# Convolution, routing and loads of a convolution-then-MoE kernel regrouped: sequences in place of half sequences, and another mix of block sizes

## The chip, the cores and the metric

The kernel runs on one core of one Trainium2 chip. The metric is the time of the core in device microseconds for one launch. The kernel before took 1353.02, 1347.88 and 1350.54 us in three runs; their median is 1350.54 us. Everything is in fp32.

The names of the engines: TensorE (PE in the profile; PEld is its weight load), VectorE (DVE), ScalarE (ACT), GpSimd (POOL) and SyncE (SP, which here only issues DMAs).

## The reference

Eight sequences of 3584 tokens with 192 channels go through a causal convolution of seven taps, whose weights are shared by the 24 channels of a head, and then through a mixture of eight experts in which each token uses one expert.

```python
# lightweight convolution: weight is (8 heads, 7 taps)
w = softmax(weight, axis=-1)
x_pad = concatenate([zeros(B, 6, D), x], axis=1)
out[b, s, h, :] = sum_k w[h, k] * x_pad[b, s + k, h, :]       # heads of 24 channels

# experts, x is now the convolution's output
logits = x @ w_gate                                            # (B, S, 8)
local_gate = sigmoid(x @ w_local)
for b in range(B):
    prev_e = -1
    for s in range(S):
        fresh_e = argmax(logits[b, s])
        e = fresh_e if s == 0 or local_gate[b, s] < 0.5 else prev_e
        prev_e = e
        p = softmax(logits[b, s])
        out[b, s] = p[e] * (relu(x[b, s] @ w1[e]) @ w2[e])     # 192 -> 1024 -> 192
```

A token with an open local gate takes over the expert of the token before it, so routing is a scan along the sequence. The expert's two products are nearly all of the arithmetic.

## The kernel before

**Tokens and parts.** The 28672 tokens are cut into 16 parts of `PT` = 1792, two (`PER`) for each sequence. In a part each of the 128 partitions holds `NT` = 14 consecutive tokens, and a load of a part brings six more tokens per partition (`HALO`) for the taps. `load_x` (L129) issues such a load on SP's queue, 1920 KB.

**Parts 0 and 1** are convolved on TensorE in the opening (`wide`, L210, and `wide_route`, L410), so that the first experts can start early. Nothing of that is looked at here, except that `route1`, the routing of part 1, is emitted to its end (L1254) before the first block's products.

**Parts 2 to 15** go through `conv` (L383). For each of eight heads ScalarE multiplies the first tap (L394, 128 x 336 elements) and VectorE adds the other six, one `scalar_tensor_tensor` each (L404), in place in a row tile `y_sb` in SBUF: 48 VectorE instructions per part. `ys` holds four row tiles (L111), one for each part. At the fifth head the load of the next part is issued (L401), into the other one of two buffers `xs`.

`logits` (L581) then turns the rows with four VectorE transposes (L586), multiplies by the gates on TensorE (L597, 48 small products), brings the result back with ScalarE (L602), another transpose (L605) and sixteen small copies (L613). `route` (L618) is some fifty small VectorE instructions on 14 or 112 elements per partition: which expert, the scan of the local gate over tokens, partitions and parts, the softmax, and for each token its row in a table `slots` in DRAM, where tokens of one expert lie together. `tables` (L771) follows: for each kind of block, `table` (L808) works out in 18 to 22 tiny VectorE instructions which expert and rows each block takes. 

**Scatters.** A routed part leaves fourteen entries in `to_put`. `put` (L788) takes one and lets GpSimd write 128 rows to `slots` with an indirect DMA (L795), ordered behind a given ScalarE instruction. The places of these calls are written into the loops of the blocks.

**Blocks.** The experts work on blocks of 128, 256 or 512 rows of one expert (1, 2 or 4 units). How many of each kind are certain to be full after each part is worked out when the kernel is built (`ONE`, `TWO`, `FOUR`, L64 to L67): units of 128 until part `EARLY`, 256 until part `FIRST`, then 512, and at the end pairs and single units for what is left (L912 to L916). For each block `load_w` (L926) brings the expert's weights, 1536 KB, into one of four buffers, and `load_rows` (L936) its rows from `slots`; the latter waits for the scatters of the parts that it needs. `ensure` (L1206) does this up to three blocks ahead; when a part needed soon isn't yet routed and put, it forces steps of its work.

A block of 128 or 256 rows is `hidden` (L989: products L1000, ReLU on ScalarE L1004, scatters behind it) and `output` (L1077: products L1089, ScalarE's scaled copy L1097, VectorE's scaled add L1101, GpSimd's indirect store of 128 rows L1106). A block of 512 rows uses `seven` (L1032) in place of `hidden`: seven half-size products (L1048) in place of eight by the method of Strassen and Winograd, with sums made by GpSimd before (`combine_w`, `combine_x`, L1009 to L1030), copies by ScalarE (L1053, L1057, L1059) and sums by VectorE (L1062, L1065, L1072) between them. Meanwhile the rows of the next block are turned (`turn_out`, `turn_in`, L376 and L978).

**The order.** It is written out by hand: what a function emits first runs first on its engine. Convolution and routing are generators, which emit one VectorE instruction and yield its estimated price in us. `step(time)` (L1150) is called at fixed places in a block and draws work from them until the given time is spent, routing before convolution; "pe" and "hop" mark places where routing must wait for a free PSUM bank or for another engine, and convolution fills the gap. A block of 512 calls `step` four times:

```python
SIDE = (3.6, 4.6, 3.6, 3.6)
LEAD = 2
```

`step(SIDE[0])` stands ahead of L1062, `step(SIDE[1])` ahead of `output`, and the other two ahead of the two passes of L1101. Smaller blocks call it with 2.1, 1.2 and 1.3 us (128 rows) or 4.6, 1.2 and 3.6 us (256 rows). Convolution of a part starts (`start_conv`, L1121) when its predecessor's is done, when it is no more than `LEAD` parts ahead of routing, and when no scatter of the part three before waits:

```python
free = not any(p[0] <= g - 3 for p in to_put)
```

## Time and profile before

| what | value |
|---|---|
| median of three runs | 1350.54 us |
| the profiled execution's own time | 1407.22 us |
| its span in the profile | 1405.5 us |
| mean granted clock of TensorE | 0.98 |
| VectorE, convolution's taps (L404), 672 instructions | 398.1 us, mean 604 ns |
| ScalarE, first taps (L394), 112 instructions | 63.1 us, mean 581 ns |
| GpSimd, scatters to `slots` (L795), 228 instructions | 228.2 us, mean 1001 ns |
| GpSimd, stores of the output (L1106), 229 instructions | 231.6 us, mean 1011 ns |
| TensorE, `output` (L1089) / `hidden` (L1000) | 636.0 us / 354.2 us |
| DMA: weights, 112 loads of 1536 KB and 12 of 512 KB; tokens, 14 loads of 1920 KB | 201 GB/s over the span |

The profiled execution took 56.7 us longer than the median of the runs without a profile. The durations in the profile belong to the profiled execution, so a sum of them is to be compared with 1407.22 us. A group of instructions is named by its line, its engine, its operation and its tiles; busy time is the sum over the span, and instructions on different engines overlap.

### The profile page before, as it was taken

What the parts mean: (1) busy time and instruction counts of PE and PEld (TensorE: products, weight loads), DVE (VectorE), ACT (ScalarE), POOL (GpSimd) and SP (SyncE); (2) the same over time, 40 slices, a digit from 0 to 9 for tenths busy, and PEclk for the clock granted to TensorE, in tenths of its full rate; (3) what the DMA queues carried; (4) which work ended last, traced back from release to release, by engine and by line L of the source; (5) the groups of instructions that cost most, each with busy time, mean ns of one, the idle gap of its engine ahead of it and who ended that gap; (6) DMA issues with size and microseconds to landing.
All of it is one profiled execution on the core that took longest, in us unless ns stands there. A gap on an engine that the chain in (4) does not pass through costs nothing.

```text
span 1405.5 us, 41143 instructions
## 1 busy us (share of the span) xinstructions
PE 1323.0 (94%) x16474; PEld 1247.0 (89%) x16474; DVE 925.4 (66%) x2556; ACT 681.7 (49%) x1441; POOL 655.3 (47%) x759
## 2 busy tenths in 40 slices
PE   9799999899999999998989999989999799999997
PEld 8789999899989999897878887878889689999997
DVE  6879889698888978889999898995721122110000
ACT  5355555444444544445564645444444355544543
POOL 4445353343434444356665665664656644512111
PEclk9999999999999999999999999999999989999999
DMA  5799998875657666562543524233242243335893
GB/s 195 270 379 353 355 377 314 339 278 191 223 205 271 240 211 243 196 259 92 195 157 104 192 85 159 73 130 118 88 152 85 88 151 125 107 132 196 304 338 132
DMA packets 60197, 284.70 MB, mean 203 GB/s; under 512 B 11744, under 2 KB 30999, under 8 KB 43874
## 3 DMA queue, kind: packets, MB, share of 16 engines
q1 hardware_dynamic: 37680, 236.81, 47.1%
q0 software_dynamic: 22320, 45.22, 8.7%
q8 instruction: 132, 2.16, 0.6%
q14 instruction: 63, 0.52, 0.1%
q10 hardware_dynamic: 2, 0.00, 0.0%
HBM read 236.39 MB, written 46.07 MB: 201 GB/s over the span
## 4 chain that ended last, share of the span: by engine, by line
PE 75%; DVE 17%; issue 3%; ACT 2%; DMA 1%; another core or an unknown queue 0%; POOL 0%; DVEq 0%; POOLq 0%; ACTq 0%; SPq 0%
PE ps L1089 36%; PE ps L1000 23%; PE ps L1048 11%; DVE y_sb L404 6%; PE ps L376 2%; PE ps L597 1%; DVE lt L613 1%; DVE h L1065 1%; DMA xg<-slots 1%; DVE h L1062 1%; DVE o_sb L1101 1%; DVE h L1072 1%; ACT h L1057 1%; PE hps L226 1%; ACT h L1053 0%
## 5 line engine op out<-in xcount | busy, mean ns | idle before, releaser
L1089 PE MATMUL ps<-wb,h 64*128 64x192 f32 x7328 | 636.0, 326 | 8.5 <-issue 6.9
L1089 PEld LDWEIGHTS ps<-wb,h 64*128 64x128 f32 x7328 | 605.3, 188 | 16.3 <-issue 12.8
L1106 POOL DMA_INDIRECT out_dram<-o_sb,xg x229 | 231.6, 1011 | 455.0 <-DVE o_sb L1101 396.5
L404 DVE SCALAR_TENSOR_TENSOR y_sb<-x_sb,c,y_sb 128x336 f32<-128x336 f32 x672 | 398.1, 604 | 30.3 <-ACT y_sb L394 13.1
L1000 PE MATMUL ps<-xT,wb 64*128 64x128 f32 (+1 forms) x4320 | 354.2, 314 | 4.4 <-issue 2.3
L1000 PEld LDWEIGHTS ps<-xT,wb 64*128 64x128 f32 x4320 | 332.8, 188 | 16.2 <-issue 7.7
L795 POOL DMA_INDIRECT slots<-y_sb,posi x228 | 228.2, 1001 | 226.7 <-ACT h L1073 77.9
L1101 DVE SCALAR_TENSOR_TENSOR o_sb<-ps,xg,o_sb 128x192 f32<-128x192 f32 x229 | 87.3, 413 | 309.5 <-ACT o_sb L1097 303.4
L1097 ACT ACTIVATE o_sb<-ps,xg 128x192 f32<-128x192 f32 x229 | 86.8, 418 | 323.0 <-PE ps L1089 316.3
L1004 ACT ACTIVATE h<-ps 128x256 f32<-128x256 f32 (+1 forms) x360 | 148.2, 464 | 193.0 <-PE ps L1000 112.8
L978 ACT COPY xT<-ps 128x128 f32<-128x128 f32 (+2 forms) x464 | 194.1, 418 | 13.7 <-PE ps L376 4.4
L1048 PE MATMUL ps<-xT,wb 64*128 64x256 f32 x1248 | 151.9, 382 | 1.9 <-POOL xT L1026 1.2
L1048 PEld LDWEIGHTS ps<-xT,wb 64*128 64x128 f32 x1248 | 125.3, 191 | 14.1 <-POOL xT L1026 1.6
L376 PEld LDWEIGHTS ps<-ident,xg 64*64 64x64 f32 (+1 forms) x916 | 47.5, 127 | 30.4 <-DVE h L1062 21.7
L1048 PE MATMUL ps<-xc,wt 64*128 64x256 f32 x416 | 56.0, 387 | 18.0 <-ACT h L1057 14.1
L376 PE MATMUL ps<-ident,xg 64*64 64x64 f32 (+1 forms) x916 | 53.2, 224 | 20.9 <-DVE h L1062 16.0
L1062 DVE TENSOR_TENSOR h<-ps,h 128x1024 f32<-128x1024 f32 x26 | 31.6, 1217 | 58.2 <-PE ps L1048 56.1
L1048 PEld LDWEIGHTS ps<-xc,wt 64*128 64x128 f32 x416 | 39.2, 187 | 28.6 <-ACT h L1057 17.7
L394 ACT ACTIVATE y_sb<-x_sb,c 128x336 f32<-128x336 f32 x112 | 63.1, 581 | 0.0
L1048 PE MATMUL ps<-xc,wb 64*128 64x256 f32 x416 | 56.6, 416 | 4.2 <-ACT h L1059 3.8
L1057 ACT COPY h<-ps 128x1024 f32<-128x1024 f32 x26 | 26.3, 1012 | 63.1 <-PE ps L1048 57.6
L1048 PEld LDWEIGHTS ps<-xc,wb 64*128 64x128 f32 x416 | 45.4, 205 | 11.7 <-issue 8.2
(266 smaller groups left out, 1036.1 us busy)
## 6 DMA issues: line engine op xcount, KB each, us to landing
wb<-in_w_dram SPq DMA_DIRECT2D x112, 1536.0 KB
x_sb<-in_x_dram SPq DMA_DIRECT2D x14, 1920.0 KB
xg<-slots SPq DMA_DIRECT2D x26, 390.0 KB
xg<-slots SPq DMA_DIRECT2D x35, 195.0 KB
wb<-in_w_dram SPq DMA_DIRECT2D x12, 512.0 KB
xg<-slots SPq DMA_DIRECT2D x53, 97.5 KB
out_dram<-o_sb,xg POOLq DMA_INDIRECT x229
slots<-y_sb,posi POOLq DMA_INDIRECT x228
```

The source lines that it names most:

```text
L376: nc.tensor.transpose(to, src[rows], identity=ident[rows, rows])
L394: nc.scalar.activation(cols(h), chans(h, 0), Act.Copy, scale=c[:, h, 0:1])
L404: nc.vector.scalar_tensor_tensor(cols(h), chans(h, k), c[:, h, k:k + 1], cols(h), Alu.mult, Alu.add)
L795: ins = nc.gpsimd.indirect_dma_start(out=slots[:, :], in_=rows, in_offset=None, out_offset=bass.IndirectOffsetOnAxis(ap=to, axis=0)).ins
L978: copied = nc.scalar.copy(a, b)
L1000: nc.tensor.matmul(hps[:, half, j, :], lhsT=wb[rows, f0:f0 + P], rhs=xT[rows, d, :], start=(d == 0 and j == 0), stop=(d == KD - 1), skip_g ...
L1004: relu = nc.scalar.activation(hT[two][:, half], hps[:, half], Act.Relu)
L1048: nc.tensor.matmul(to[:, half, j, :], lhsT=b[rows, j * P:(j + 1) * P], rhs=a[rows, :], start=(first and j == 0), stop=True, skip_group_che ...
L1089: nc.tensor.matmul(yps[:, half, k * D:(k + 1) * D], lhsT=h[two][rows, side, j, k * P:(k + 1) * P], rhs=wb[rows, WA + f * D:WA + (f + 1) * ...
L1097: nc.scalar.activation(o_sb[:, k, :], yps[:, 0, k * D:(k + 1) * D], Act.Copy, scale=xg[:, at + k, 0:1])
L1101: nc.vector.scalar_tensor_tensor(o_sb[:, k, :], yps[:, 1, k * D:(k + 1) * D], xg[:, at + k, 0:1], o_sb[:, k, :], Alu.mult, Alu.add)
L1106: sent = nc.gpsimd.indirect_dma_start(out=out, in_=o_sb[:, k, :], in_offset=None, out_offset=bass.IndirectOffsetOnAxis(ap=xg.bitcast(I32)[ ...
```

## The change

1. *Groups.* The parts from the fifth on are convolved, routed and tabled two at a time, that is, by sequences. `GROUPS` is 0, 1, 2, 3, 5, 7, ..., 15: a sequence has the number of its second part. `NS` = 28 tokens per partition in place of 14. Convolution has 28 x 24 = 672 elements in each instruction, routing 28 or 224; the charges (`yield`) grow from 0.6 to 1.0 for a tap and by 0.12 for most steps of `route`. `logits` still transposes and multiplies part by part, and joins the two at the transpose of L605 and the copies of L613. The scan of the local gate then never crosses a part inside a sequence.
2. *Loads.* The tokens lie in memory as (sequence, half of the heads, token, 96 channels). A load brings half of the heads of a part (parts 2 and 3) or of a sequence, and convolution goes by such units (`UNITS`). It is issued in the third of the four heads of the unit before it. The extra load at block `LATE` = 3 is gone, and `LEAD` too.
3. *Row tiles.* `ys` has two tiles of twice the size in place of four. A convolution starts when the scatters of the sequence two before have been emitted.
4. *Blocks.* `EARLY` goes from 3 to 4 and `FIRST` from 8 to 6.
5. *Scatters.* `more` emits a second `put` while more than 14 rows wait, after the three places in `seven` and after the ReLUs in `hidden`.
6. *Budgets.* `SIDE` is (3.0, 4.0, 3.0, 3.0). The last part of `route1` (the tables of part 1) is emitted after the first block's `output`, and that block has other budgets.

The diff, cut to its core:

```diff
-EARLY = 3
+EARLY = 4
...
-FIRST = 8
+FIRST = 6
...
+GROUPS = [*range(EARLY)] + [*range(EARLY + 1, NPART, 2)]
+ONE = {g: _sure(min(g + 1, EARLY) * PT, UT) for g in GROUPS}
...
-    ys = ctx.enter_context(tc.tile_pool(name="ys", bufs=4))
+    ys = ctx.enter_context(tc.tile_pool(name="ys", bufs=2))
...
+    def load_x(g, hh):
+        x_sb = x_tile()
+        n, skip = (NT, g % PER * PT) if g < EARLY else (NS, 0)
+        src = x[g // PER, hh]
+        win = bass.AP(tensor=src.tensor, offset=src.offset + skip * DH,
+                      ap=[[n * DH, P], [1, (n + HALO) * DH]])
+        nc.sync.dma_start(out=x_sb[:, :n + HALO, :].rearrange("p t d -> p (t d)"), in_=win)
         return x_sb
...
-        return ys.tile([P, NB, DG], F32, name="y_sb")
+        return ys.tile([P, 2 * NB, DG], F32, name="y_sb")
...
+    def conv(u, x_sb):
+        g, hh = UNITS[u]
+        if hh == 0:
+            got[g] = rows_in(g)
+        y_sb = got[g]
+        n = NT if g < EARLY else NS
...
-        first(0)
+        heads = range(hh * H // 2, (hh + 1) * H // 2)
+        first(heads[0])
         yield 0
-        for h in range(H):
-            if h + 1 < H:
+        for h in heads:
+            if h + 1 in heads:
                 first(h + 1)
-            if h == H // 2 and 2 < g < NPART - 1:
-                x_in[g + 1] = load_x(g + 1)
+            if h == heads[2] and u + 1 < len(UNITS):
+                x_in[UNITS[u + 1]] = load_x(*UNITS[u + 1])
             for k in range(1, KC):
...
-                yield 0.6
+                yield 0.6 if n == NT else 1.0
...
+        parts = n // NT
+        ls = sm.tile([P, 2, 2, TQ * Q], F32, name="ls", bufs=1)
...
+        for part in range(parts):
+            zt = z_tile()
...
+            for half in range(2):
+                nc.scalar.copy(ls[:, half, part, :], lps[half])
+            yield "hop"
...
+    def more(behind):
+
+        if len(to_put) > NT:
+            put(behind)
+
+    def puts_by(behind):
+        put(behind)
+        more(behind)
...
             for _ in range(shares[two] if n == 2 else (0, sum(shares))[two]):
                 put(relu)
+            if n == 2 or two:
+                more(relu)
...
-        put(nc.scalar.copy(h11, xb))
+        puts_by(nc.scalar.copy(h11, xb))
...
-        put(nc.scalar.copy(h22, yb))
+        puts_by(nc.scalar.copy(h22, yb))
...
-        put(nc.scalar.activation(h12, h12, Act.Relu))
+        puts_by(nc.scalar.activation(h12, h12, Act.Relu))
...
-            step(1.2 if n < KT else SIDE[2 + part], wps_p if n < KT else None)
+            step((1.2 if n > 1 or st["block"] else 0) if n < KT else SIDE[2 + part],
+                 wps_p if n < KT else None)
...
-    SIDE = (3.6, 4.6, 3.6, 3.6)
-    LEAD = 2
-    LATE = 3
+    SIDE = (3.0, 4.0, 3.0, 3.0)
+    LATER = GROUPS[2:]
+    UNITS = [(g, hh) for g in LATER for hh in range(2)]
...
     def start_conv():
-        g = st["conv"] + 1
-
-        free = not any(p[0] <= g - 3 for p in to_put)
-        if (st["cgen"] is None and g < NPART and g <= st["route"] + LEAD and free
-                and (g != 3 or g in x_in and st["block"] > LATE + 2)):
-            st["conv"] = g
-            st["cgen"] = conv(g, x_in.pop(g))
-            next(st["cgen"])
+        u = st["unit"] + 1
+        if st["cgen"] is None and u < len(UNITS) and UNITS[u] in x_in:
+            last = UNITS[u][0] // PER * PER - PER - 1
+            if st["routed"] >= last and not any(p[0] <= last for p in to_put):
+                st["unit"] = u
+                st["cgen"] = conv(u, x_in.pop(UNITS[u]))
+                next(st["cgen"])
...
-    rest(route1)
+    next(route1)
     start.close()
...
-        if i == LATE:
-            x_in[3] = load_x(3)
...
-        step({1: 2.1, 2: 4.6, 4: SIDE[1]}[n], zps_p if n == KT else xps_p)
+        step(2.4 if i == 0 else {1: 2.1, 2: 4.6, 4: SIDE[1]}[n], zps_p if n == KT else xps_p)
         output(n, wbs.pop(i), xgs.pop(i), hT)
+        if i == 0:
+            rest(route1)
```

The rest of the diff gives the small tiles of `route` 28 columns and takes `n` of them, and lets `tables` and `blocks` run over `GROUPS`.

## The prediction

> **What bounds the kernel now.** I read the page first, then stretches of the span one by one, then the chain of waits in two of them, then single blocks. The first two lines are the page's shares and its slices of 1/40 of the span.
>
> ```profile
> PE 1323.0 (94%) x16474; PEld 1247.0 (89%) x16474; DVE 925.4 (66%) x2556; ACT 681.7 (49%) x1441; POOL 655.3 (47%) x759
> PE   9799999899999999998989999989999799999997
> DVE  6879889698888978889999898995721122110000
> DMA  5799998875657666562543524233242243335893
> ```
>
> TensorE is busy throughout, so what the kernel can gain is TensorE's work itself and the few per cent in which it waits. The windows view says where those lie. Its columns are the length, then busy time (and instructions) of PE, PEld, DVE, ACT and POOL, the granted clock, the DMA share and GB/s.
>
> ```profile
> 48.00:262.00 214.00, 202.73 (x3208) 196.88 (x3210) 183.34 (x556) 111.62 (x350) 95.62 (x94) 1.00 0.91 345
> 267.00:620.00 353.00, 346.78 (x4166) 332.17 (x4167) 293.94 (x922) 162.62 (x369) 137.85 (x136) 0.99 0.66 229
> 624.00:957.00 333.00, 305.44 (x3595) 275.31 (x3594) 301.52 (x694) 170.30 (x249) 209.51 (x234) 0.96 0.39 137
> 957.00:1132.00 175.00, 153.69 (x1644) 142.35 (x1629) 68.90 (x195) 77.70 (x107) 103.92 (x124) 0.96 0.32 106
> 1132.00:1245.00 113.00, 113.00 (x1290) 107.05 (x1288) 26.06 (x37) 59.48 (x83) 53.59 (x67) 1.00 0.33 115
> ```
>
> These are the blocks of 128 rows, of 256, and three stretches of the blocks of 512. TensorE waits mostly in the third and fourth. In the third VectorE is 91% busy and looks like the bound; in the fourth it is 39% busy and TensorE waits as much. So VectorE is not the whole story. The chain of waits (start, length, what) in an undisturbed block of 512, and in one of the fourth stretch:
>
> ```profile
> 1142.99 7.77 PE ps L1048 x72
> 1150.76 0.46 PE ps L376 x14
> 1173.42 10.40 PE ps L1089 x128
> ...
> 1066.60 3.92 PE ps L1048 x24
> 1070.53 1.01 ACT h L1057
> ```
>
> An undisturbed block takes 1193.84 - 1173.42 = 20.42 us (successive starts of its 10.40 us of L1089). In the disturbed one L1057 waits for products that take 3.92 us where the other's pace gives 24 x 0.108 = 2.6. The timeline of POOL at that moment:
>
> ```profile
> 1061.87 0.98 POOL L795 DMA_INDIRECT slots<-y_sb,posi  x1
> 1063.15 0.99 POOL L1106 DMA_INDIRECT out_dram<-o_sb,xg  x1 [0.30 <-issue]
> 1064.45 0.99 POOL L1106 DMA_INDIRECT out_dram<-o_sb,xg  x1 [0.30 <-issue]
> 1065.74 0.97 POOL L1106 DMA_INDIRECT out_dram<-o_sb,xg  x1 [0.31 <-issue]
> 1067.02 0.97 POOL L1106 DMA_INDIRECT out_dram<-o_sb,xg  x1 [0.30 <-issue]
> 1068.30 0.96 POOL L795 DMA_INDIRECT slots<-y_sb,posi  x1 [0.31 <-issue]
> ```
>
> Six scatters back to back; without L795 the same block has two pairs of L1106 and no wait. Blocks with four L795 and an idle VectorE take 23.40 us, +2.98 (from 1053.24, from 1076.64), the mildest 22.23 (from 1031.01), and the one with ten (from 1100.04) 32.38, +12.0. I can't say why scatters make products late; that they go together is what I use.
>
> **What the Trainium skill says.** "VectorE: DVE Perf Modes", section "The TRN2 errata": a fixed latency per instruction, (N+151)/0.96 ns for a two-input fp32 operation. For the convolution's N = 336 that is an estimate of 507 ns; the trace has 490 at least and 570 as the median, so the fixed part is at least as large as the page's. "SBUF — State Buffer", section "SBUF: two separate sides": VectorE with two SBUF inputs and GpSimd exclude each other for a whole instruction. The trace agrees: beside GpSimd's sums (689 to 697 us) one L404 takes 945 ns, elsewhere (300 to 312 us) 570.
>
> ```profile
> L404 DVE SCALAR_TENSOR_TENSOR y_sb<-x_sb,c,y_sb 128x336 f32<-128x336 f32 x10 | 9.3, 945 | 0.3
> L404 DVE SCALAR_TENSOR_TENSOR y_sb<-x_sb,c,y_sb 128x336 f32<-128x336 f32 x18 | 10.0, 570 | 0.5
> ```
>
> "TensorE: Matmul & The Clock Gate", Part 1: an idle TensorE falls to half clock for 3.4 us at a time; the clock column's 0.96 above fits. Same page, "Architectural detail": ScalarE is a strict FIFO, so a wait of its first tap stops what is behind; no line here tests that alone.
>
> **The change, part by part.**
>
> *Blocks.* The formulas give 35 blocks of 128 rows at the start, 31 of 256, 26 of 512 and then 4 + 20 before; 49, 10, 33 and the same 24 after. An undisturbed block costs 5.45 us (1331.15 to 1336.60), 10.67 (456.90 to 467.57) and 20.42. So +14 x 5.45 - 21 x 10.67 + 7 x 20.42 = **-4.8 us**. The early blocks of 128 rows are slower than those at the end, with DMA at 0.91: the 23 from 94.04 to 229.45 us take 135.4, less two products of L597 at 2.1 (29.5/14) each, 5.70 apiece. 14 x 0.25 = **+3.5**. The 353 us of the second stretch hold 31 x 10.67 + 5 x 2.1 = 341.3; 12 lost, 0.38 a block, and 21 blocks go: **-8.0**.
>
> *VectorE.* 672 convolution steps become 96 at 336 elements and 288 at 672. The transposes give the slope: 949 - 534 = 415 ns for 384 elements, so 363 for 336. Mean 604 becomes 967: 96 x 0.604 + 288 x 0.967 = 336 us for 406, -70. Bounds for one long step: 857 (the page's formula) and 1208 (nothing fixed), -101 to 0. Routing has 73 small instructions per part, 17.1 us (lines 605 to 766 together 239 us over 14 parts); eight passes in place of fourteen, six of them some 2.4 us longer (twelve operations of 112 elements more at 1.08 ns, and the rest), come to 151, -88. Tables fall from 18 to 12 at 3.9 each, -24. Some 180 of 925 us go, and at nothing as such: TensorE's time covers VectorE's.
>
> *What that is worth.* A block of 512 gave VectorE 3.6 + 4.6 + 3.6 + 3.6 = 15.4 us of this work beside its own 3 x 1.22 + 4 x 0.41 = 5.3: 20.7 in 20.42. Now 13.0 + 5.3 = 18.3, so L1062 and L1101 are no longer late in its queue. But the fourth stretch says that with VectorE free the scatters still cost. I went through the calls of `step` and `put` with their charges (a sequence: 48 x 1.0 + 26.8; budgets 4.6, 9.4 and 13.0 a block). Done with the code of before this puts the last scatters in its 20th or 21st block of 512, where the trace has them (1100 to 1125 us). After, scatters run through 25 of 33: eleven blocks with four, seven with seven (`puts_by` and `more` double them while over 14 wait), one in which `ensure` forces seven, six with none to two; eight follow undisturbed. Before, 26 blocks took 621.3 us (623.4 to 1244.7): 530.9 + 10.5 for L597 and 79.9 lost. After I take 2.7 for a block with four (between 1.8 and 3.0), 3.6 for one with seven (bounds 2.7, if a longer burst adds nothing, and 7 x 1.2 = 8.4 at the rate of the ten), 8 for the forced one, 1 for each of seven others: 30 + 25 + 8 + 7 = 70. **-9.9**, bounds -36 and +24.
>
> *Loads.* A load is now one half of the heads, issued twelve steps before the half that needs it. In the first stretch a load took 15 us from issue (121.9) over its first packet (129.9) to its last (136.8, packet records). Half a part needs half of the 7, so 11.5; half a sequence (34 against 20 rows, half the channels: 0.85 of the bytes) 14. Twelve steps last 1.3 to 2.4 blocks, 8 to 13 us. ScalarE's first tap then waits 1 to 4 us, six times before block 49, with its ReLUs and copies behind it, 13 in all. TensorE holds about one block half of work ahead: I take **+8**, bounds 0 and 24. In the first 60 us the smaller load frees DMA that nothing waits for: 0.
>
> *Row tiles.* Two of them hold four parts, as four held one each. A half of a sequence now starts when the last scatter of two sequences ago has been emitted, not a part earlier, so its first tap can wait for that scatter's read (about 2 us at POOL) on ScalarE. Five such places: **+3**, between 0 and 10. Splitting route 1 takes some 3.7 us of VectorE work (52.4 to 56.1) from in front of the first block's L1101; L1089 waited 1.5 us at 60.08: **-1.7**, bounds 0 and -3.
>
> Sum: -4.8 + 3.5 - 8.0 - 9.9 + 8 + 3 - 1.7 = -9.9. The profiled execution takes 1407.2 us and would take 1397; the runs' median is 56.7 below it, and I carry the difference over: 1350.5 - 9.9 = **1341 us**.
>
> **The rivals.** *Relief is complete*: scatters cost little once VectorE is not late, 44 lost in place of 70: 1315. For it: the blocks just before 700 us with four scatters take 21.7 (686.18 to 707.91). Against: the idle VectorE of the fourth stretch. *Loads in halves are late*: all six times 4 us uncovered, +24 in place of +8: 1357. For it, DMA at 0.91; against, the loads are smaller. *Scatter bursts, the slower side*: in the blocks of 512 `puts_by` makes bursts of nine on POOL. At 1.2 us a scatter, the rate of the block at 1100, seven blocks lose 8.4 each, the others 3.0: 59 + 33 + 8 + 4 = 104 for 70, **1375**. It decides from 5.0 us in a block with seven scatters on, where the loss is again 80. That VectorE's work doesn't shrink is no rival: the counts are fixed.
>
> **How the numbers follow.** Within 0.5% (6.8 us) counts as no change. The forecast 0.45 (own range 1330 to 1350; 0.35 of it faster, 0.10 the same), complete relief 0.17, late loads 0.13 (0.04 of it the same, 0.09 slower), bursts 0.25. Faster 0.52, same 0.14, slower 0.34. The range, 1312 to 1372, leaves out half of the bursts' case and a little of the relief's.
>
> **What would show it.** VectorE near 745 us busy, one long L404 near 0.95 us; blocks of 512 with four L795 at 22 to 23.5 us and those with seven below 25; ScalarE idle before the convolution's first tap, released by the load of x, in the first 300 us; the last eight blocks of 512 at 20.42. Wrong if a block with four scatters takes 20.4, or one with seven over 26, or if TensorE starves between 60 and 310 us.

## The result, and the profile after

The changed kernel took 1358.28 us (median of 4; 1357.39 to 1359.05) beside 1350.74 us for the kernel before: ratio 1.0057, 95% interval 1.0036 to 1.0077. A later comparison gave 1358.11 beside 1345.55 us, 1.0087 (1.0064 to 1.0109). The time lies inside the range on record, but on the side of slower; the forecast was faster by 9.9 us.

The kernel before took 1345 to 1348 us (median) in two of five later sets of runs and 1406 to 1415 us in the other three; one chip gave both. Below, *cheap* and *dear* conditions stand for these two kinds, since a scatter costs TensorE more time in the second. Every ratio here is taken within one set. The profile shown before the prediction, of an execution of 1407.22 us, has the length of the dear kind. The profiled execution of the changed kernel took 1357.90 us, close to its median. A second profile of the kernel before, of an execution of 1344.23 us (experiment e1), is therefore the one to compare with. Its windows view follows; the columns are as before (length, busy time of PE, PEld, DVE, ACT, POOL, clock, DMA share, GB/s). The rows are its blocks of 128, of 256, the passage (the last block of 256 rows, in which the first block of 512 is prepared), the blocks of 512, and two of them late in the kernel, with four and with seven scatters while VectorE has no convolution or routing left.

```profile
52.05:253.25 201.20, 193.11 (x3155) 190.24 (x3150) 176.92 (x528) 111.11 (x346) 89.02 (x89) 1.00 0.93 356
253.25:594.75 341.50, 339.45 (x4277) 323.25 (x4273) 293.60 (x925) 164.27 (x374) 140.85 (x138) 1.00 0.70 245
594.75:614.28 19.53, 17.93 (x271) 15.50 (x266) 19.07 (x27) 12.82 (x19) 15.06 (x17) 1.00 0.78 275
614.28:1187.60 573.32, 547.43 (x6365) 509.38 (x6362) 382.89 (x909) 299.93 (x429) 359.56 (x413) 0.99 0.38 132
...
1008.65:1029.07 20.42, 20.42 (x234) 19.25 (x232) 5.06 (x7) 11.23 (x16) 14.27 (x17) 1.00 0.36 126
1049.49:1069.91 20.42, 20.42 (x234) 19.25 (x232) 5.07 (x7) 11.24 (x16) 16.47 (x20) 1.00 0.13 46
```

The last two rows are the surprise: 20.42 us, the undisturbed time, with PE busy in all of it. In the first profile such blocks took 22.2 to 25 us and the one with ten scatters 32.38. The same stretches of the changed kernel, a block of 128 rows in it, and two late blocks of 512:

```profile
51.03:359.20 308.17, 280.20 (x4619) 273.66 (x4614) 257.13 (x672) 158.88 (x485) 146.06 (x126) 0.99 0.90 338
359.20:466.93 107.73, 107.73 (x1369) 103.69 (x1370) 84.04 (x182) 50.51 (x110) 62.13 (x52) 1.00 0.76 275
466.93:493.05 26.12, 17.49 (x175) 15.47 (x171) 17.91 (x17) 12.29 (x17) 22.48 (x20) 0.80 0.64 234
493.05:1201.30 708.25, 689.70 (x8178) 649.61 (x8176) 377.97 (x705) 380.82 (x524) 473.76 (x523) 0.99 0.39 132
204.15:210.90 6.75, 5.66 (x84) 5.52 (x85) 6.57 (x9) 3.55 (x11) 4.47 (x3) 1.00 0.98 349
961.14:981.56 20.42, 20.42 (x236) 19.29 (x234) 5.06 (x7) 11.23 (x16) 16.27 (x20) 1.00 0.44 150
981.56:1001.97 20.41, 20.41 (x234) 19.16 (x232) 5.06 (x7) 11.22 (x16) 14.23 (x17) 1.00 0.35 119
```

TensorE idles 28.0 us in the blocks of 128 (308.17 - 280.20), where the kernel before idled 8.1. In the blocks of 256 it idles 2.0 of 341.5 us there and not at all here. In the passage to the first block of 512 TensorE works 17.5 of 26 us, at a mean granted clock of 0.80. The page of the changed kernel:

```profile
PE 1285.3 (95%) x16754; PEld 1227.2 (90%) x16754; DVE 785.5 (58%) x1736; ACT 696.4 (51%) x1408; POOL 756.9 (56%) x823
PE   9889998988999979998999899999999999999997
DVE  6878898895886885796848765386212212200000
DMA  4898999898885752445325533333425432345883
...
L428 DVE SCALAR_TENSOR_TENSOR y_sb<-x_sb,c,y_sb 128x672 f32<-128x672 f32 (+1 forms) x384 | 335.0, 881 | 39.3 <-ACT y_sb L417 29.9
L833 POOL DMA_INDIRECT slots<-y_sb,posi x228 | 257.4, 1129 | 105.8 <-issue 49.2
...
L417 ACT ACTIVATE y_sb<-x_sb,c 128x672 f32<-128x672 f32 (+1 forms) x64 | 49.5, 793 | 16.5 <-issue 7.7
```

VectorE is relieved: 785.5 us in place of 925.4 in the first profile. GpSimd went the other way, 756.9 for 655.3: a scatter (L833) now takes 1129 ns in the mean, 1001 before, and the seven more blocks of 512 bring 63 more of its sums (the 297 take 245 us; the 234 of the first profile took 180). ScalarE's first tap (L417, 16.5 us of idle time) now waits; before, L394 had 0.0 in that place.

For the table below each interval from one block's first product of `output` to the next block's is taken, and from it what it takes undisturbed (5.45, 10.67 and 20.42 us; 2.6 + 5.47 and 5.2 + 10.02 where the size changes) and 2.1 us for the products of the gates of each part. What is left is lost.

| lost, us | first profile of before | second (e1) | changed | e2 | e3 | e4 | e10 | e12 |
|---|---|---|---|---|---|---|---|---|
| blocks of 128 | 17.0 | 9.6 | 34.0 | 22.5 | 36.8 | 35.2 | 29.1 | 16.7 |
| passage to 256 | 1.7 | 1.4 | 0.0 | 1.6 | 0.0 | 0.0 | 0.0 | 0.0 |
| blocks of 256 | 14.9 | -0.6 | -0.6 | 8.1 | -0.6 | -0.6 | -0.6 | 44.8 |
| passage to 512 | 4.0 | 2.2 | 10.9 | 12.7 | 8.9 | 11.2 | 10.8 | 10.8 |
| blocks of 512 | 75.7 | 38.5 | 26.3 | 48.3 | 50.3 | 20.6 | 26.3 | 1.4 |

Changed against e1: +24.4, -1.4, 0, +8.7 and -12.2, with -4.8 for the undisturbed blocks and -1.0 at the start: +13.7 us, which is the difference of the two spans (1356.2 - 1342.5). The medians differ by 7.5 and 12.6 us in the two comparisons; this execution of the kernel before was one of its shorter ones. A second trace of the changed kernel (e9) gives 34.5, 0.0, -0.6, 11.1 and 25.3. Two places therefore pay for what the blocks of 512 gain: the blocks of 128 rows and the passage.

**Blocks of 128 rows.** VectorE's timeline in one of them (start, length, what):

```profile
203.59 0.41 DVE L1151 SCALAR_TENSOR_TENSOR o_sb<-ps,xg,o_sb 128x192 f32<-128x192 f32 x1
203.92 6.51 DVE L428 SCALAR_TENSOR_TENSOR y_sb<-x_sb,c,y_sb 128x672 f32<-128x672 f32 x7
210.34 0.41 DVE L1151 SCALAR_TENSOR_TENSOR o_sb<-ps,xg,o_sb 128x192 f32<-128x192 f32 x1
```

Between two blocks' L1151 stand seven long steps, 6.51 us; with L1151 the block can't be shorter than 6.75. `step` draws until its budget is spent, and the last step may overrun it. So 2.1, 1.2 and 1.3 us at a charge of 1.0 draw 3, 2 and 2 steps: 7.0 us for a budget of 4.6. At 0.6 the same budgets drew 4, 2 and 3 steps of 0.57 us, 5.1 in all, which fit into 5.45.

A second loss there, in ScalarE's timeline and then GpSimd's:

```profile
329.07 1.22 ACT L1025 COPY xT<-ps 128x128 f32<-128x128 f32 x4
338.00 0.87 ACT L417 ACTIVATE y_sb<-x_sb,c 128x672 f32<-128x672 f32 x1 [7.71 <-issue]
338.90 0.42 ACT L1146 ACTIVATE o_sb<-ps,xg 128x192 f32<-128x192 f32 x1
```

```profile
330.73 0.96 POOL L833 DMA_INDIRECT slots<-y_sb,posi  x1 [0.30 <-issue]
340.05 1.08 POOL L1156 DMA_INDIRECT out_dram<-o_sb,xg  x1 [8.35 <-DVE offs L788]
```

By the code, the scatter at 330.73 is the last out of the row tile that L417 is to write; the profile itself names no releaser here ("issue"). By the packet records the packets of this scatter and of the one at 329.46 start between 333.4 and 336.8 us, among packets of a load of weights, so up to 6 us after the issue; L417 starts at 338.00. That the wait is for the row tile is tested in e10. Behind L417 stand the scaled copy and the ReLUs of the next block; this block and the next lose 6.2 and 1.7 us.

**The passage.** The chain of waits of the changed kernel:

```profile
465.97 1.64 POOL out_dram L1156
...
469.81 0.96 POOL slots L833
...
473.61 0.96 POOL slots L833
474.57 0.03 issue
474.60 1.40 POOL wt L1063
...
481.44 1.23 POOL xT L1075
482.67 0.04 issue
482.71 8.26 PE ps L1097 x56
```

GpSimd works almost without a break: two stores, four scatters, then its sums, and TensorE's products wait for these until 482.71. A sum takes 1.2 to 1.4 us here; in the second profile of the kernel before the 234 sums of this kind take 0.73 in the median and never more than 1.06. The traces show what VectorE's steps have to do with it. Sums with no convolution step beside them take 0.73 us in the median in both kernels. The 63 sums that overlap a short step (e1) take 0.87, the 68 that overlap a long one (changed kernel) 1.22, up to 1.46. The steps lengthen too: short ones from 0.57 to 0.92 us beside sums, long ones from 0.92 to 1.27. So both engines wait in both kernels, and GpSimd's part grows from 0.14 to 0.49 us a sum. In the passage the six sums that TensorE waits for take 3.4 us more than at 0.73 each, and the four scatters ahead of them hold GpSimd for 4.8 us.

### The profile page after: what moved, and what is told of

It is laid out like the page before. It is cut to its first block, busy times and chain, and to the rows that moved or that the text cites. A ratio compares the mean times of both kernels' runs of the same rounds, so it can differ in the third digit from the quotient of the medians.

```text
span 1356.2 us, 40960 instructions
## 1 busy us (share of the span) xinstructions
PE 1285.3 (95%) x16754; PEld 1227.2 (90%) x16754; DVE 785.5 (58%) x1736; ACT 696.4 (51%) x1408; POOL 756.9 (56%) x823
## 4 chain that ended last, share of the span: by engine, by line
PE 59%; DVE 8%; POOL 3%; issue 2%; DMA 2%; ACT 1%; SPq 0%; POOLq 0%; DVEq 0%; ACTq 0%
PE ps L1138 29%; PE ps L1097 20%; PE ps L1047 8%; DVE y_sb L428 2%; PE ps L385 1%; POOL slots L833 1%; PE ps L627 1%; ACT xT L1025 1%; DVE o_sb L1151 1%; DVE lt L644 1%; DMA wb<-in_w_dram 1%; POOL out_dram L1156 0%; DMA xg<-slots 0%; DMA slots<-y_sb,posi 0%; DMA out_dram<-o_sb,xg 0%
## 5 line engine op out<-in xcount | busy, mean ns | idle before, releaser
L1138 PE MATMUL ps<-wb,h 64*128 64x192 f32 x7328 | 624.2, 325 | 20.6 <-DVE o_sb L1151 10.7
L428 DVE SCALAR_TENSOR_TENSOR y_sb<-x_sb,c,y_sb 128x672 f32<-128x672 f32 (+1 forms) x384 | 335.0, 881 | 39.3 <-ACT y_sb L417 29.9
L833 POOL DMA_INDIRECT slots<-y_sb,posi x228 | 257.4, 1129 | 105.8 <-issue 49.2
L1151 DVE SCALAR_TENSOR_TENSOR o_sb<-ps,xg,o_sb 128x192 f32<-128x192 f32 x229 | 87.6, 412 | 369.8 <-ACT o_sb L1146 369.4
L1047 PE MATMUL ps<-xT,wb 64*128 64x128 f32 (+1 forms) x3984 | 275.5, 291 | 6.6 <-issue 3.5
L1047 PEld LDWEIGHTS ps<-xT,wb 64*128 64x128 f32 x3984 | 266.0, 189 | 10.6 <-issue 7.7
L1097 PE MATMUL ps<-xT,wb 64*128 64x256 f32 x1584 | 194.2, 385 | 20.2 <-POOL xT L1075 18.6
L1025 ACT COPY xT<-ps 128x128 f32<-128x128 f32 (+2 forms) x464 | 194.1, 418 | 12.2 <-PE ps L385 5.4
L1051 ACT ACTIVATE h<-ps 128x256 f32<-128x256 f32 (+1 forms) x332 | 120.9, 417 | 149.0 <-PE ps L1047 113.7
L1097 PEld LDWEIGHTS ps<-xT,wb 64*128 64x128 f32 x1584 | 156.3, 192 | 39.1 <-POOL xT L1075 19.9
L1097 PE MATMUL ps<-xc,wt 64*128 64x256 f32 x528 | 70.7, 388 | 0.0
L1063 POOL TENSOR_TENSOR wt<-wb 128x256 f32<-128x256 f32 x33 | 25.5, 772 | 67.0 <-PE ps L1097 66.5
L417 ACT ACTIVATE y_sb<-x_sb,c 128x672 f32<-128x672 f32 (+1 forms) x64 | 49.5, 793 | 16.5 <-issue 7.7
L1112 ACT ACTIVATE h<-h 128x1024 f32<-128x1024 f32 x33 | 34.9, 1057 | 40.3 <-DVE h L1111 40.3
```

What stands on the lines that cost most here:

```text
L417: nc.scalar.activation(cols(h), chans(h, 0), Act.Copy, scale=c[:, h, 0:1])
L428: nc.vector.scalar_tensor_tensor(cols(h), chans(h, k), c[:, h, k:k + 1], cols(h), Alu.mult, Alu.add)
L833: ins = nc.gpsimd.indirect_dma_start(out=slots[:, :], in_=rows, in_offset=None, out_offset=bass.IndirectOffsetOnAxis(ap=to, axis=0)).ins
L1025: copied = nc.scalar.copy(a, b)
L1047: nc.tensor.matmul(hps[:, half, j, :], lhsT=wb[rows, f0:f0 + P], rhs=xT[rows, d, :], start=(d == 0 and j == 0), stop=(d == KD - 1), skip_g ...
L1051: relu = nc.scalar.activation(hT[two][:, half], hps[:, half], Act.Relu)
```

## The experiments

**e1: the kernel before once more.** No edit.

> The kernel before, unchanged, for a second profile. Theory A: the 57 us by which its first profiled execution exceeded the median belong to that one execution, and with them the late products beside scatters. Then the second profile has a span near 1349 us, and its blocks of 512 with four scatters and an idle VectorE (from about 1000 us on) take 20.4 us in place of 22.2 to 25. Rival: they come with every profile of this kernel; then the span is again near 1400 us and those blocks take 22 us and more. The time is 1350 us either way.

1346.43 us (median of 12) beside 1348.15, the same program. The span of the profile was 1342.5 us and late blocks with four scatters took 20.42 us (rows above). So the surplus of the first profile belongs to that execution, which is theory A. That it comes with conditions and not with profiling is shown by the dear sets, in which unprofiled runs of the kernel before took 1406 us too. What makes scatters dear in these stays open.

**e2: five long steps in a block of 128 rows in place of seven.**

```diff
-            step((1.2 if n > 1 or st["block"] else 0) if n < KT else ...
+            step((1.2 if n > 1 else 1.0 if st["block"] else 0) if n < KT else ...
-        step(2.4 if i == 0 else {1: 2.1, 2: 4.6, 4: SIDE[1]}[n], ...
+        step(2.4 if i == 0 else {1: 2.0, 2: 4.6, 4: SIDE[1]}[n], ...
```

> The changed kernel with budgets 2.0, 1.0 and 1.3 us in blocks of 128 rows in place of 2.1, 1.2 and 1.3, so that five long convolution steps are drawn in a block in place of seven (short ones stay nine). Theory: seven steps of 0.94 us are 6.6 us of VectorE in a block of 5.45 us, and nine such blocks took 6.75 us. Then these blocks return to 5.45 us; 9 x 1.3 = 12 us less, some of it given back where convolution is late afterwards: 1346 to 1352 us, 1347 taken. Rival: the blocks are held by loads or scatters, not by VectorE's budget; then the time stays at 1358 us and the blocks at 6.7.

1379.73 us beside 1348.15, ratio 1.0228 (1.0204 to 1.0252): slower. A block of five steps, and then a block of 512 later on, in the windows view of e2:

```profile
213.34:218.79 5.45, 5.45 (x91) 5.45 (x88) 5.24 (x7) 3.54 (x10) 4.13 (x4) 1.00 1.02 394
537.95:582.24 44.29, 30.83 (x427) 26.56 (x424) 35.01 (x118) 13.53 (x22) 24.15 (x27) 0.83 0.29 102
```

The first part holds: 5.45 us, and the blocks of 128 lose 22.5 in place of 34.0, 11.5 us less where 12 were expected. But the block at 537.95 takes 44.29: the rows of a sequence are needed that isn't routed yet, and `ensure` puts 35 us of VectorE's work and twelve scatters into it. So the seven steps were not only a rounding error. VectorE's early work is due at a date, and what isn't done among the blocks of 128 is paid for later: 11.5 us gained, and 34 lost in the rows below it in the table (1.6 + 8.7 + 1.8 + 22.0).

**e3: no second scatters.**

```diff
     def more(behind):
-        if len(to_put) > NT:
-            put(behind)
+        return
```

> The changed kernel without the second scatters (more does nothing). Theory: in three blocks of 512 six scatters in a row stand in GpSimd's queue ahead of the sums for the next block's products, and TensorE waits 7 to 11 us for these; with three in a row the wait is 3 us or none. 15 to 20 us less there, with some given back where convolution waits longer for its row tile or rows are forced out: 1340 to 1356 us, 1348 taken. Rival: bursts do no harm (blocks with seven scatters and an idle VectorE take 20.42 us), and what matters is that the row tile comes free in time; then it is slower than 1358 us, by up to 20.

1384.57 us, 1.0271 (1.0247 to 1.0296). The rival holds, and the loss is larger than it said: rows come out too late; one block of 512 (539.34 us) has sixteen scatters forced into it and takes 48.44. The passage still loses 8.9. One late block is of use below. VectorE has nothing left but the block's own work in it (5.07 us), and twelve scatters in a row, from 1039.07 to 1053.96 us, stand ahead of GpSimd's sums:

```profile
1044.41:1068.75 24.34, 22.41 (x234) 20.62 (x233) 5.07 (x7) 11.26 (x16) 18.42 (x22) 0.93 0.60 214
```

The sums take 0.72 to 0.75 us each, and yet TensorE waits for them: 3.9 us are lost to the scatters' place in the queue, with no long step near.

**e4: GpSimd's sums ahead of the last pair of scatters** in blocks of 512: the scatters behind the last ReLU are emitted after `combine_w` and `combine_x`.

```diff
-        puts_by(nc.scalar.activation(h12, h12, Act.Relu))
+        last = nc.scalar.activation(h12, h12, Act.Relu)
...
                 wt, xc = combine_w(wbs[i + 1]), combine_x(xT)
+            if n == KT:
+                puts_by(last)
```

> The changed kernel with as many scatters, but in blocks of 512 the pair behind the last ReLU is emitted after GpSimd's sums for the next block and not before. Theory of GpSimd's queue: the sums start 2 x 1.3 to 2 x 1.9 us earlier in the blocks where they are late; four such places: 8 to 14 us less, 1347 us taken, and the blocks of 29.2 and 27.3 us become 26 and 24. Rival (scatters hurt wherever they stand, or VectorE's lock stretches the sums): no change within 3 us.

1353.82 us, 1.0052 (1.0036 to 1.0069): against the changed kernel's 1.0057 and 1.0087 in other sets, no certain difference in time. The blocks say more. GpSimd's timeline of e4 at the block that took 29.17 us:

```profile
624.43 0.97 POOL L1156 DMA_INDIRECT out_dram<-o_sb,xg  x1 [0.30 <-DVE y_sb L428]
625.71 0.97 POOL L833 DMA_INDIRECT slots<-y_sb,posi  x1 [0.30 <-issue]
...
629.52 0.96 POOL L833 DMA_INDIRECT slots<-y_sb,posi  x1 [0.30 <-issue]
630.51 1.39 POOL L1063 TENSOR_TENSOR wt<-wb 128x256 f32<-128x256 f32 x1
```

Four scatters ahead of the sums where there were six, and this block takes 25.93 in place of 29.17, and 29.31 in the second trace of the changed kernel: 3.2 to 3.4 us less, as two scatters less ahead of the sums should give. The one of 27.28 takes 24.51, but it took 25.66 in that second trace without the edit. The blocks of 512 lose 20.6 in place of 26.3 and 25.3.

**e5: the new mix of blocks in the kernel before.**

```diff
-EARLY = 3
+EARLY = 4
...
-FIRST = 8
+FIRST = 6
```

> The kernel before with EARLY = 4 and FIRST = 6 alone: the new mix of blocks with convolution and routing still by parts. Theory of lead: this mix asks for the rows of parts 6 to 9 earlier, when VectorE has not delivered them, and work is then forced in front of TensorE (about 31 us of VectorE work in the last block of 256 rows, of which 20 are uncovered). Undisturbed blocks give -4.8, fourteen more blocks of 128 rows some +4, the forced one +15 to +25: 1360 to 1372 us, 1365 taken. Rival: the mix is harmless and only the grouping by sequences costs; then 1343 to 1350 us.

1452.72 us beside 1406.42, so in dear conditions: 1.0328 (1.0304 to 1.0353), more than twice the loss expected. The last block of 256 rows (459.43 to 503.45 us) holds 41.5 us of VectorE's work and takes 44.0 us, 28.8 lost, somewhat more than the 15 to 25 expected of it; the blocks of 512 lose 109.6 us. The mix asks for rows that half-sequence work at its old pace doesn't deliver.

**e12: the grouping with the old mix.** The mirror of e5: blocks of 128 rows for three parts, of 256 for eight, the rest as changed.

```diff
+ONES = 3
...
-FIRST = 6
+FIRST = 8
...
-ONE = {g: _sure(min(g + 1, EARLY) * PT, UT) for g in GROUPS}
+ONE = {g: _sure(min(g + 1, ONES) * PT, UT) for g in GROUPS}
```

> The changed kernel with the mix of blocks of the kernel before (35, 31 and 26): grouping by sequences without the new mix. Theory of lead: the rows of parts 4 and 5 are asked for by the first block of 256, some 75 us earlier than in the changed kernel, and come only with the whole sequence; about 58 us of VectorE work is then forced in one block: 1.025 to 1.045 times the kernel before. Rival (the grouping as such costs nothing in lead): ratio 0.99 to 1.01.

1369.42 us beside 1345.55: 1.0182 (1.0156 to 1.0209), less than expected. The forced work of some 58 us came, as 37.9 and 20.5 us of VectorE's time in two blocks, partly beside TensorE's products. Windows of e12, the first block of 256 rows and the next:

```profile
269.30:317.50 48.20, 19.89 (x318) 15.83 (x312) 37.94 (x64) 8.18 (x19) 31.98 (x25) 0.68 0.49 184
317.50:339.96 22.46, 10.88 (x120) 10.17 (x121) 20.49 (x78) 10.51 (x21) 5.71 (x6) 0.84 0.57 219
```

Here the rows of parts 4 and 5 are asked for and come only when the whole sequence is routed; 45 us are lost in these two blocks. The passage loses 10.8 us, as in the changed kernel. The 26 blocks of 512 lose 1.4 us together, but convolution ends at 697.5 us, with the first of them, and VectorE has only routing and tables left in five more; so e12 doesn't show what long steps cost all through the blocks of 512. Neither half of the change pays alone, though e5 and e12 were measured under different conditions.

**e6, e14, e17: the change's budgets in the kernel before.**

```diff
-    SIDE = (3.6, 4.6, 3.6, 3.6)
+    SIDE = (3.0, 4.0, 3.0, 3.0)
```

> The kernel before with SIDE = (3.0, 4.0, 3.0, 3.0) alone, the budgets of the change. In its second profile blocks of 512 lose 38.5 us beside VectorE's own 21 to 23 us each; with 22 convolution steps for 26 and less routing a block they should lose some 15 less, with 2 forced scatters more: 1330 to 1340 us, 1335 taken. Rival (VectorE's order and not its amount, or work that comes back later, sets the loss): within 4 us of 1348.

> The kernel before with the change's budgets (3.0, 4.0, 3.0, 3.0) alone, a second time, in case the kernel before takes some 1348 us here. It then loses 38.5 us in its blocks of 512, all of it where VectorE is busy for 21 us and more; five convolution steps less a block are 2.9 us: 15 to 20 us less, and two or four forced scatters more at 3 to 10 us: ratio 0.988 to 0.996, 0.992 taken. Rival (what is not done there comes back as forced work in full): ratio 0.998 to 1.003.

> The kernel before with the change's budgets alone. Where the kernel before takes some 1348 us: ratio 0.988 to 0.996, 0.992 taken, as expected of e14. Rival: what is left undone comes back as forced work, 0.998 to 1.003. Where it takes 1406 us or more, 0.992 to 0.997 as in the two trials before.

Ratios 0.9918 (0.9898 to 0.9938), 0.9966 (0.9950 to 0.9982) and 0.9933 (0.9909 to 0.9957), all three where the kernel before takes 1406 to 1415 us. It is a gain each time, of 12.2, 6.0 and 9.4 us by the medians. Its place is not shown: the blocks of 512 lose 63.5 us in e6, but 73.7 in e14 and 74.2 in e17, for 75.7 in the first profile, which is of another set. Part of the work comes back, as the rival said: in each of the three one block takes 31 us, with as much of VectorE's work in it, and a late one with twelve scatters 36.0 to 37.6. Whether the budgets gain anything in cheap conditions stays open.

**e7, e16: GpSimd's sums first, in the last block of 256 rows too.** On top of e4, `hidden` keeps its ReLUs in a list when the next block has 512 rows:

```diff
+            if later is not None:
+                later.append(relu)
+                continue
...
                 puts_by(last)
+            elif n_next == KT:
+                for relu in relus:
+                    puts_by(relu)
```

> The changed kernel with GpSimd's sums ahead of the last pair of scatters in blocks of 512, and in the last block of 256 rows ahead of all four behind its ReLUs. That block and the next lose 11 us together in the changed kernel, with GpSimd busy without a break. Theory of GpSimd's queue: 4 x 1.6 us less there, and 5.7 us in the blocks of 512 as measured: 12 us less than the changed kernel, ratio 0.997 to 1.001 to the kernel before, 0.998 taken. Rival (the first sums wait for something else): the first block loses 11 us as before, ratio 1.002 or more.

> The kernel of e7 (GpSimd's sums ahead of the last scatters, also in the last block of 256 rows) a second time, in case the kernel before takes some 1348 us here. Theory of GpSimd's queue: the passage loses 5 to 7 us in place of 11, the blocks of 512 some 20 in place of 26: ratio 1.000 to 1.004, 1.001 taken. Rival: the passage loses 11 us as before, ratio 1.005.

1.0119 (1.0094 to 1.0143) and 1.0122 (1.0087 to 1.0156), both in dear conditions; the ratios say nothing on the edit, since the changed kernel itself wasn't run in these. The passage loses 7.1 and 6.6 us, with four scatters less ahead of the sums; without the edit it lost 10.9 and 11.1 in cheap conditions. In the kernel before the passage loses more in the dear profile (4.0) than in the cheap one (2.2), so the conditions don't explain the smaller loss.

**e8, e15, e18: the blocks of 512 later** in the changed kernel; e15 and e18 with the edit of e10 too.

```diff
-FIRST = 6
+FIRST = 8
```

> The changed kernel with FIRST = 8 as before it: 24 blocks of 256 rows and 26 of 512 in place of 10 and 33. Undisturbed blocks cost 14 x 10.67 - 7 x 20.42 = 6.4 us more. Theory: the change's losses in the blocks of 512 and at the passage to them (37 us) come from doubled scatters and forced work that fall together with long convolution steps; with the blocks of 512 starting 150 us later most of that falls into blocks of 256, which have room: 37 becomes 12 to 20. Sum -10 to -19: ratio 0.993 to 1.000, 0.996 taken. Rival (blocks of 256 then lose as much): ratio 1.005 to 1.012.

> The changed kernel with FIRST = 8 and the later start of convolution of e10, two edits of the schedule. Blocks +6.4 us; passage 11 to 6; blocks of 512 25 to 10; tile -5: -18 in all against the changed kernel, ratio 0.993 to 0.999 to the kernel before, 0.996 taken. Rival (twos lose in place of the blocks of 512): ratio 1.002 or more.

> The changed kernel with FIRST = 8 and the later start of convolution. Where the kernel before takes some 1348 us: blocks +6.4 against the changed kernel, ones 29 lost, passage 6, blocks of 512 about 8: ratio 0.994 to 1.000, 0.997 taken. Rival (the blocks of 512 lose 20 as in the changed kernel): 1.003 or more. Where it takes 1406 us or more, 0.995 as in e15.

0.9952 (0.9933 to 0.9970), 0.9953 (0.9937 to 0.9970), 0.9949 (0.9924 to 0.9973), again only in dear conditions. There it beats the kernel before by 0.5%, with 41.1, 50.7 and 46.1 us lost in the blocks of 512 for the 75.7 of the first profile, and 41 to 44 in the blocks of 128 for 17.0. That is no more than the new budgets alone gave the kernel before in the same conditions. In cheap conditions, in which the changed kernel was measured, it was not run.

**e9: the changed kernel again**, as a measure for e10 to e12.

> The changed kernel, unchanged, beside its variants, since the two sets of runs so far stand on two chips, on which the kernel before takes 1348 and 1406 us. If the kernel before takes 1348 us here, the ratio is 1.006 as in the first comparison. If it takes 1406, the theory that each scatter in a block of 512 costs time there says 1.010 to 1.020, since the changed kernel has 105 scatters in its blocks of 512 and the one before some 80.

1358.11 beside 1345.55 us. (The chip is that of e5 to e8, where the kernel before took 1406.42; so it is not the chip alone that decides what it takes.)

**e10: no first tap right behind the scatters of its row tile.**

```diff
+            rested = blocks[st["block"]][1] > 1 or st["block"] > put_at.get(last, -9) + 1
-            if st["routed"] >= last and not any(p[0] <= last for p in to_put):
+            if st["routed"] >= last and rested and not any(p[0] <= last for p in to_put):
```

(`put` notes the block of each group's last scatter in `put_at`.)

> The changed kernel in which, in blocks of 128 rows, a convolution doesn't start in the block of the last scatter that frees its row tile or in the next, but one later. Theory: ScalarE's first tap stands in its queue waiting for that scatter's read (3.8 us at 222 us and 7.7 us at 338 us), with ReLUs and copies behind it, and TensorE loses 2 + 8 us. Then both waits go, VectorE starts two blocks later: 6 to 8 us less than the changed kernel beside it. Rival (TensorE loses there for another reason): no change, or slower by what VectorE delivers late.

1353.43 for 1358.11 us beside each other: 4.7 us less, ratio 1.0055 (1.0035 to 1.0074) for 1.0087. The loss in the blocks of 128 falls by 5.4 against e9's 34.5, and ScalarE no longer stands still at 330 us. So the first tap did stand there for the row tile, and what is behind it on ScalarE with it. The gain is below the 6 to 8 us expected; a block at 226 us now loses 3.9 where it lost 2.4.

**e11, e13: more lead, and smaller doses.** 77 blocks of 128 rows, 10 of 256 and 26 of 512 (the expectation counted 76 and 11), five long steps, and second scatters among the blocks of 128 at any length of the list; e13 with the edit of e10 besides. The edits of e12, with six parts in place of three, and of e2, and:

```diff
-        if len(to_put) > NT:
+        if len(to_put) > (NT if blocks[st["block"]][1] > 1 else 0):
```

> The changed kernel with more lead and smaller doses: blocks of 128 rows for all that is certain after part 6 (76 in place of 49), FIRST = 8 (11 of 256, 26 of 512), five long convolution steps in a block of 128 in place of seven, and second scatters there at any length of the list. Undisturbed blocks cost 1209.0 for the changed kernel's 1199.3. Theory: in the schedule nothing is forced any more, so that the shorter doses, which alone made it 22 us slower, now give their 11 us, the passage to 512 loses 4 for 11 and the blocks of 512 about 10 for 26: -18 in all, ratio 0.988 to 0.997 to the kernel before. Rival (the doses are not what costs; more blocks of 128 rows lose 0.7 each to loads of weights and scatters): ratio 1.01 or more.

> The kernel of e11 (more lead, five steps) with the start of convolution two blocks after the last scatter out of its row tile, as in e10. In e11 three first taps of ScalarE waited 9.4, 9.6 and 8.6 us for the tile, and TensorE lost 6.6 + 2 in each of these places. Theory: these go, 15 to 22 us less than e11: ratio 0.992 to 0.999 to the kernel before if e11's 1.0098 is its base, 0.995 taken. Rival (TensorE waits in these places for work of VectorE that is late as well): ratio 1.005 or more.

e11: 1356.07 beside 1345.55, 1.0098 (1.0059 to 1.0136): the expected gain didn't come. Passage 6.0 and blocks of 512 7.7 lost, about as expected, but the blocks of 128 lose 38.9: the wait for the row tile appears three times, with 9.4, 9.6 and 8.6 us on ScalarE. e13: 1442.93 beside 1413.89, 1.0216 (1.0182 to 1.0250). Of ScalarE's three waits one of 6.8 us is left, but these are dear conditions; many blocks of 128 have three or four scatters, as in e11, and these blocks lose 72.3 us in place of 38.9. It doesn't tell what e13 does in cheap conditions.

## Why the prediction was wrong

*What failed first* is a sentence of the part on VectorE: "Some 180 of 925 us go, and at nothing as such: TensorE's time covers VectorE's". In blocks of 512 it is nearly so. In blocks of 128 rows it is not: a dose of seven steps of 0.94 us is longer than the block. The charges were gone through for `step` and `put`, but the number of steps drawn in a block of 128 was never multiplied by the new duration. The term "+3.5" for these blocks was to be +24.4. Of these, 11.5 went with smaller doses (e2) and 5.4 with a later start on the row tile (e10); 4.0 is an estimate for fourteen more blocks at the loss of the second profile (9.6/34 each); the other 3.5 are not assigned. By e2 the large doses aren't a mere slip: with smaller ones the rows are late.

*The base* failed as well. The 79.9 us lost in blocks of 512 and the 12 in blocks of 256 were read from an execution 56.7 us above the median, and this difference was carried over as if the median's run lost the same. The second profile has 40.7 (38.5 and 2.2, with the passage) and nothing in the blocks of 256. So the term -8.0 for these is 0.

*Blocks*: -4.8, as forecast; the durations recur to 0.01 us.

*Blocks of 512*: -9.9 was forecast with the passage in it; -3.5 came (-12.2 and +8.7). The wrong price was that of scatters. "Wrong if a block with four scatters takes 20.4" was the test set, and it came true: with VectorE idle, blocks with four to seven scatters take 20.42 us. The price of 2.7 was one of the dear conditions: in e8, measured in these, blocks with four scatters and VectorE idle take 21.8 to 25.0 us. In cheap conditions scatters cost where many stand ahead of GpSimd's sums: 5 to 11 us in three places in each trace of the changed kernel, with long steps running, and 3.9 in e3 with VectorE idle. The rival "scatter bursts" named this queue's nine scatters but charged them through late products, everywhere.

*Loads by halves*: +8 was forecast; ScalarE waited 2.3 us for `x_sb` in all, in two places. The loads of half the channels came in time. That this term of +8 failed and the -8.0 above did too is chance: the two errors cancel. No run takes the loads alone back.

*Row tiles*: +3 was forecast, 0 to 10; some 5 came. The place and the waiting instruction were right. The scatter's packets start up to 6 us after its issue and the tap 7.3 us after it, not 2: the forecast took GpSimd's part and left out the wait of the packets, at a DMA share of 0.9.

*Route 1*: -1.7 was forecast. The start is 1.0 earlier (51.03 for 52.05) and in the repeat 0.2 later (52.25), while the second block, which now holds the deferred tables, loses 2.3 to 2.5: no gain.

*VectorE*: 785.5 us for "near 745". Seven more blocks of 512 bring 21 sums of 1.22 us, 25.6, which the sum left out; long steps take 985 ns in the mean, not 967, +5; some 10 us are not assigned. The lower bound of 857 ns for a long step was too low: its median is 919. With 570 for a short one this gives 349 ns for 336 elements and, as an estimate, 221 ns that don't depend on their number.

Between -9.9 and +13.7 lie 23.6 us: 8.0 of them from the blocks of 256, 6.4 from the blocks of 512 with their passage, 0.7 from the start, 16.5 from the blocks of 128 (24.4 - 1.4, less the 3.5 and 3 of the forecast), and -8 from the loads. What the Trainium skill says in "SBUF — State Buffer", section "SBUF: two separate sides", a lock held for a whole instruction, was cited for VectorE's steps alone. Its other side was left out: beside steps of 0.92 us GpSimd's sums take 1.22 us in the median, beside steps of 0.57 us 0.87, with none 0.73. This agrees with the page; no run takes this wait away alone.

## What to carry to other kernels

Before a profile is priced, hold its own time against the median; where they differ by 4%, take no loss from it until a second profile has it. When work that is drawn in doses gets longer instructions, count the doses again for every kind of block, the shortest first: each budget can overrun by up to one instruction. And a larger group delivers later: ask by what date each consumer needs the first of it, since work moved off a busy stretch is cheap only if it isn't due there.

## What was not expected of the hardware

- The same program took 1341 to 1353 us in some sets and 1400 to 1421 in others, on one chip both. In the first profile, which has the length of the second kind, a block of 512 with four scatters and VectorE idle takes 23.40 us (23.55 in e14, of a dear set, with other budgets) in place of 20.42. Why is open.
- GpSimd's sum of 128x256 elements takes 0.73 us with no convolution step beside it, 0.87 in the median (at most 1.06) beside VectorE's steps of 0.57 us, and 1.22 (at most 1.46) beside steps of 0.92. Steps of either length take 0.35 us more beside sums.
- The packets of a scatter of 128 rows of 780 bytes, which holds GpSimd for 0.96 us, started up to 6 us after its issue, between those of a load of weights.
